# Norm products of the gate and value weights ordered behind attention scores, their squares in four buffers, and w_out's word conversion ordered behind the second token group

## The chip, the core and the metric

The kernel runs on one core of a Trainium2 chip. The metric is the device time of one execution in microseconds. Three runs of the kernel before took 2195.69, 2197.92 and 2199.4 us; their median is 2197.92 us.

## The reference, cut to what matters

Three stages follow one another. The second stage's weights arrive as float64 words in memory (each value is a pair of 32-bit words) and have to be turned into float32 first.

```python
scores = scale * (q @ k.T)                       # 4 batches, 8 heads, 576 x 576, head width 64
scores = where(scores >= max - tau, scores, -1e9)
x = softmax(scores) @ v                          # 2304 tokens x 512

xn = x / rms(x) * rms_g
x = (silu(xn @ w_gate) * (xn @ w_val)) @ w_out   # 512 -> 1536 -> 512

P = sinkhorn(exp(x @ moe2_w_gate), 8 rounds)     # 2304 x 8 experts
out = sum over e of P[:, e] * (relu(x @ w1[e]) @ w2[e])   # 512 -> 1024 -> 512
```

## The kernel before, in words

**Attention.** A batch has 36 tiles: four query groups of 128 rows times 8 heads, and four tiles that hold the 64 remaining rows of two heads each. `att_tile` computes one tile's scores on PE (line 282, four matmuls of 288 columns into one of two PSUM buffers), takes the row maximum on DVE (line 292), the exponential on ACT (line 296), mask and sum on DVE (line 298), splits the result into two 16-bit halves on ACT and POOL (lines 303 to 305), and has SP transpose them by DMA (line 307). Three tiles later `att_values` multiplies the transposed tile with v on PE (line 330); an ordering edge holds these matmuls behind the newest scores. After eight tiles `end_main` divides by the sums (line 376) and `finish_x` normalises the token group, ending with line 353 on DVE; the group, 128 tokens, is then transposed by DMA into `xnT`.

**Preparing the gate and value weights.** When the second token group (number 1) is finished in program order, which is at tile 18, the program emits `prep_group` three times. Each calls `prep_in` for w_gate and for w_val, so there are six calls of four blocks (128x512) each, 24 blocks in all. Per block, `words` loads the 64-bit words by DMA, `to_f32` joins them (ACT line 432, DVE lines 433, 435, 436), ACT squares the result (line 456) and PE multiplies the squares with the squared gains (line 457) to get column norms. The fourth product of a call closes the sum; DVE takes its maximum (line 459), a scale follows, and the four blocks are converted to two 16-bit halves (ACT line 465, DVE line 466). The blocks wait in `stage`, three areas of four blocks that share memory with `wo`, so call number n+3 reuses the area of call n. The squares use tag `u`, two buffers.

**Preparing w_out.** `prep_out` loads 12 blocks of words into the tags `x2` and `x2t`, one buffer each, in turn; `to_f32` joins them (the DVE instructions write the tile `wol`), ACT squares and sums them (line 490). When all 12 are done a common scale is found, and DVE, ACT and POOL write the two halves block by block (lines 507, 508, 509).

**MLP.** A pair of token groups j goes through `mlp_in(j)` (line 530, 288 matmuls for 12 hidden blocks, each followed by ACT line 538, DVE lines 539 and 540, ACT line 544, POOL line 545) and `mlp_out(j)` (line 561, 72 matmuls against `wo`). There are nine pairs. The hidden tiles `tT` have four buffers, of which one pair takes three.

**What sets the order.** Each engine executes its instructions in one fixed order. A scheduler finds the orders ahead of time: it simulates the engines and at each point takes the instruction of the best priority whose inputs are there in its simulation. Priority follows the program's order, except that `attention_order` lifts attention ahead: tiles up to 18 come before the weights' preparation, later tiles come behind `prep_group` but before `mlp_in(0)`, `prep_out` and `mlp_out(0)`. `tc.issue_after(ins)` adds order edges only: each instruction traced in the block that runs on the engine of `ins` has to come behind `ins` in that engine's order. Instructions of other engines in the block are not held.

**After attention** the second expert stage runs (lines 860, 906 and 921), from 679 us to the end.

Of the kernel before, what the change touches and what calls it, by code (L numbers as in the profile page):

```python
# [7 lines left out]
F32 = mybir.dt.float32  # L8
F16 = mybir.dt.float16
BF16 = mybir.dt.bfloat16  # L10
I32 = mybir.dt.int32
AF = mybir.ActivationFunctionType
ALU = mybir.AluOpType
# [6 lines left out]
def kernel(  # L20
# [24 lines left out]
    V, A, G, T = nc.vector, nc.scalar, nc.gpsimd, nc.tensor  # L45
    B, H, S, D = q.shape
    NT, DM = out.shape
    DFF = moe_w_gate.shape[1]
    E, _, FF = moe2_w1.shape
    P = 128  # L50
    KD = DM // P
# [9 lines left out]
    def small(shape, name, dt=F32, bufs=1):  # L61
        return p0.tile(shape, dt, tag=name, name=name, bufs=bufs)
# [43 lines left out]
    gsq = small([P, KD], "gsq", BF16)  # L106
# [16 lines left out]
    HD = DM // 2  # L123
# [17 lines left out]
    pw = pw_cm.__enter__()  # L141
# [124 lines left out]
    HS = S // 2  # L266

    waiting = []
    LAG = 3

    def att_tile(st, c, heads, slot, group):

        kT = st["kT"]
        qT, qX = st["q", c]
        nm = f"{st['b']}_{c}_{heads[0]}"
        sums = group["sums"]
        sp = psa.tile([P, 2, 512], F32, tag="S", name=f"S{nm}", bufs=2)
        rows = P // len(heads)
        for qq, first in ((qT, True), (qX, False)):
            for i, h in enumerate(heads):  # L280
                for j in range(2):
                    last = T.matmul(  # L282
                        sp[i * rows : (i + 1) * rows, j, 0:HS],
                        lhsT=qq[:, h, 0:rows],
                        rhs=kT[h // H2][:, h % H2, j * HS : (j + 1) * HS],
                        start=first,
                        stop=not first,
                    )
        sv = sp[:, :, 0:HS]
        nt = pa.tile([P, 3], F32, tag="nt", name=f"nt{nm}", bufs=4)  # L290
        mx = nt[:, 2:3]
        V.tensor_reduce(mx, sv, AX.XY, ALU.max)
        A.activation(nt[:, 0:1], mx, AF.Copy, scale=st["wt"][:, c : c + 1])
        e = pa.tile([P, S], F32, tag="e", name=f"e{nm}", bufs=3)
        ev = e.rearrange("p (a n) -> p a n", a=2)
        A.activation(ev, sv, AF.Exp, bias=nt[:, 0:1], scale=st["c2"][:, c : c + 1])  # L296
        A.activation(nt[:, 1:2], mx, AF.Identity, bias=st["bt"][:, c : c + 1])
        V.scalar_tensor_tensor(  # L298
            ev, sv, nt[:, 1:2], ev, ALU.is_ge, ALU.mult, accum_out=sums[:, slot : slot + 1]
        )  # L300

        hl = pa.tile([P, 2 * S], F16, tag="hl", name=f"hl{nm}", bufs=3)
        A.activation(hl[:, 0:S], e, AF.Copy)  # L303
        G.tensor_tensor(hl[:, S + REM :], e[:, 0 : NCH * P], hl[:, 0 : NCH * P], ALU.subtract)  # L304
        G.tensor_tensor(hl[:, S : S + REM], e[:, NCH * P :], hl[:, NCH * P : S], ALU.subtract)
        eT = pa.tile([P, 2 * S // P, P], F16, tag="eT", name=f"eT{nm}", bufs=3)
        nc.sync.dma_start_transpose(out=eT, in_=hl)
        waiting.append((st, heads, slot, group, eT))
        if len(waiting) > LAG:

            with tc.issue_after(last.ins):
                att_values(*waiting.pop(0))
# [25 lines left out]
        return rs  # L338

    xnT = {}  # L340

    def finish_x(i, x, ivx):

        ssq = pa.tile([P, 1], F32, tag="ssq", name=f"ssq{i}", bufs=2)
        xn = pa.tile([P, 2, DM], F16, tag="xn", name=f"xn{i}", bufs=1)
        A.activation(xn[:, 0, :].bitcast(BF16), x, AF.Square, scale=ivx, accum_out=ssq)
        ms = pa.tile([P, 1], F32, tag="ms", name=f"ms{i}", bufs=2)
        V.tensor_scalar(ms, ssq, 1.0 / DM, 1e-6, ALU.mult, ALU.add)
        rs = pa.tile([P, 1], F32, tag="rs", name=f"rs{i}", bufs=2)
        G.tensor_tensor(rs, ms, mhalf, ALU.pow)  # L350
        V.tensor_scalar(rs, rs, 16.0, ivx, ALU.mult, ALU.mult)
        A.activation(xn[:, 0, :], x, AF.Copy, scale=rs[:, 0:1])
        V.scalar_tensor_tensor(xn[:, 1, :], x, rs[:, 0:1], xn[:, 0, :], ALU.mult, ALU.subtract)
        j, o = i // 2, (i % 2) * P
        if o == 0:
            xnT[j] = pw.tile([P, 2 * KD, 2 * P], F16, tag="xnT", name=f"xnT{j}", bufs=2)
        nc.sync.dma_start_transpose(
            out=xnT[j][:, :, o : o + P], in_=xn.rearrange("p l d -> p (l d)")
        )
# [49 lines left out]
    wo32 = wo.rearrange("p k l f -> p k (l f)").bitcast(F32)  # L409
# [14 lines left out]
    def to_f32(dst, word, name):  # L424

        lw = pw.tile([P, 2, 2, HD], F16, tag="xs", name=name, bufs=2)  # L430
        lw = lw.rearrange("p o l n -> p (o l n)").bitcast(I32)
        A.activation(dst, word[:, :, 1].bitcast(F32), AF.Copy, scale=2.0**-112)
        V.tensor_scalar(lw, word[:, :, 0], 29, None, ALU.logical_shift_right)
        di = dst.bitcast(I32)
        V.scalar_tensor_tensor(lw, di, 3, lw, ALU.logical_shift_left, ALU.bitwise_or)
        V.scalar_tensor_tensor(
            di, word[:, :, 1], -(2**31), lw, ALU.bitwise_and, ALU.bitwise_or
        )
        return lw

    staged = [0]

    def prep_in(src, w, gi, name):

        bits = src.bitcast(I32)
        raw = stage[:, staged[0] % 3]
        staged[0] += 1
        ps = psm.tile([P, DM], F32, tag="mm", name=f"{name}n{gi}")
        cols = slice(gi * DM, (gi + 1) * DM)
        for kk in range(KD):  # L450
            wd = words(
                bits[kk * P : (kk + 1) * P, 2 * gi * DM : 2 * (gi + 1) * DM], f"{name}w{gi}_{kk}"
            )
            to_f32(raw[:, kk], wd, f"{name}l{gi}_{kk}")
            sq = pw.tile([P, 2 * P], F32, tag="u", name=f"{name}q{gi}_{kk}", bufs=2).bitcast(BF16)
            A.activation(sq, raw[:, kk], AF.Square)
            T.matmul(ps, lhsT=gsq[:, kk : kk + 1].to_broadcast([P, P]), rhs=sq, start=kk == 0, stop=kk == KD - 1)
        n2 = small([P, 1], name + "n2", bufs=2)
        V.tensor_reduce(n2, ps, AX.X, ALU.max)
        s, inv = norm_scale(n2, 1, 9, f"{name}{gi}")  # L460
        gs = small([P, KD], f"{name}gs{gi}")
        V.tensor_scalar(gs, g_sb, s[:, 0:1], None, ALU.mult)
        for kk in range(KD):
            sk, hi = gs[:, kk : kk + 1], w[:, 0, kk, cols]
            A.activation(hi, raw[:, kk], AF.Copy, scale=sk)
            V.scalar_tensor_tensor(w[:, 1, kk, cols], raw[:, kk], sk, hi, ALU.mult, ALU.subtract)
        return inv
# [14 lines left out]
    def prep_out():  # L482

        bits = moe_w_out.bitcast(I32)
        n = KF // NG
        om = small([P, KF], "om")
        for f in range(KF):
            wd = words(bits[f * P : (f + 1) * P, :], f"wo{f}", ("x2", "x2t")[f % 2])
            sq = to_f32(wo32[:, f], wd, f"wol{f}").bitcast(BF16)[:, 0:DM]
            A.activation(sq, wo32[:, f], AF.Square, accum_out=om[:, f : f + 1])  # L490
        for _ in range(2):
            V.tensor_tensor(
                om.rearrange("p (g f) -> p g f", g=NG),
                om.rearrange("p (g f) -> p g f", g=NG),
                igv.to_broadcast([P, NG, n]),
                ALU.mult,
            )
        om1 = small([P, 1], "om1")
        V.tensor_reduce(om1, om, AX.X, ALU.max)
        s, inv = norm_scale(all_max(om1, "womx"), 1, 9, "wout")  # L500
        V.tensor_scalar(ixs, inv, 2.0**10, None, ALU.mult)
        sf = small([P, NG], "wosf")
        V.tensor_scalar(sf, igv, s[:, 0:1], None, ALU.mult)
        rr = pw.tile([P, 4, HD], F32, tag="x2", name="wof")
        for f in range(KF):
            r = rr[:, f % 2 * 2 : f % 2 * 2 + 2].rearrange("p o d -> p (o d)")
            V.tensor_scalar(r, wo32[:, f], sf[:, f // n : f // n + 1], None, ALU.mult)
            A.activation(wo[:, f, 0, :], r, AF.Copy)
            G.tensor_tensor(wo[:, f, 1, :], r, wo[:, f, 0, :], ALU.subtract)
# [108 lines left out]
    for b in range(B):  # L618
        for c in range(NW):
# [4 lines left out]
            i = tiles.index((b, c)) if c < NCH else tiles.index((b, None)) if b % 2 else None  # L624
# [4 lines left out]
    def prepare(b, o):  # L629

        st = states[b]
        if o < NCH * H and o % H == 1:
            prep_q(st, o // H + 1)
        if b > 0 and o in (LAG - 3, LAG - 1):
            prep_v(st, (o - LAG + 3) // 2)
        if b + 1 == B:
# [33 lines left out]

    for t in range(len(row) + LAG):
        before = tc.cur_priority
# [14 lines left out]
        for g in done:  # L687
            i = g["i"]
# [292 lines left out]
```

## Time and profile before

| | us |
|---|---|
| median of three runs | 2197.92 |
| profiled execution, its own time | 2195.02 |
| span of its instructions | 2193.2 |
| PE busy, x13872 matmuls | 2032.0 (93%) |
| DVE busy | 1490.2 (68%) |
| ACT busy | 870.9 (40%) |
| POOL busy | 471.0 (21%) |

The busy times are unions of the instructions' spans on an engine, over the whole span. Shares over the whole span hide that the stages differ, so the prediction reads stretches of the first 600 us. The times of the rows below count from the first instruction of the span.

### The profile page before, as it was taken

How to read it: one execution, taken by the hardware profiler on the slowest of the kernel's cores; microseconds unless marked ns; L12 is line 12 of the kernel's file. 1: busy time of each engine (PE TensorE's matmuls, PEld its weight loads, DVE VectorE, ACT ScalarE, POOL GpSimd, SP SyncE). 2: the span in 40 equal slices, each digit the busy share in tenths (PEclk: the TensorE clock that was granted, in tenths of full speed). 3: DMA queues.
4: the chain of work that ended last, by engine and by line, in shares of the span. 5: the costliest groups of instructions: out<-in, count | busy, mean ns of one | idle time of the engine just before them, and what ended most of it. 6: DMA issues, size and time to landing. Idle time of an engine off the chain costs nothing.

```text
span 2193.2 us, 35334 instructions
## 1 busy us (share of the span) xinstructions
PE 2032.0 (93%) x13872; PEld 1194.7 (54%) x13872; DVE 1490.2 (68%) x3026; ACT 870.9 (40%) x1774; POOL 471.0 (21%) x572
## 2 busy tenths in 40 slices
PE   1358789899999999999999999999999999999999
PEld 0236667666876755545555555555555555555554
DVE  6999677777744287865775765766757757666554
ACT  6878778877843243311221221222212212222111
POOL 1347556665743231000000000000000000000000
PEclk9859999999999999999999999999999999999999
DMA  9895879867826051000100100100001001000001
GB/s 267 207 201 100 169 145 174 159 144 115 147 55 142 18 144 40 29 30 1 39 20 20 39 20 20 39 20 20 20 20 39 20 20 39 20 20 1 1 28 60
DMA packets 321879, 154.10 MB, mean 70 GB/s; under 512 B 278960, under 2 KB 292400, under 8 KB 321712
## 3 DMA queue, kind: packets, MB, share of 16 engines
q1 hardware_dynamic: 321120, 151.82, 30.4%
q8 instruction: 108, 1.77, 0.3%
q14 instruction: 59, 0.48, 0.1%
q0 software_dynamic: 64, 0.00, 0.0%
q10 hardware_dynamic: 528, 0.02, 0.0%
HBM read 68.18 MB, written 12.98 MB: 37 GB/s over the span
## 4 chain that ended last, share of the span: by engine, by line
PE 70%; DVE 2%; DMA 1%; SPq 1%; POOL 0%; issue 0%; ACT 0%; DVEq 0%; ACTq 0%
PE y L906 33%; PE h L860 28%; PE gv L530 5%; PE x L561 2%; PE pv L330 1%; DMA w1r<-in_moe_w_dram 1%; SPq L762 0%; PE S L282 0%; DMA x2T<-x2d 0%; DVE w L714 0%; DMA w2r<-in_moe_w_dram 0%; DMA eT<-hl 0%; PE logits L804 0%; DVE w1m L725 0%; POOL xh L601 0%
## 5 line engine op out<-in xcount | busy, mean ns | idle before, releaser
L860 PE MATMUL h<-x2T,w 128*128 128x384 f16 x4032 | 703.8, 326 | 9.9 <-DMA x2T<-x2d 3.9
L860 PEld LDWEIGHTS <-w 128*128 128x128 f16 x4032 | 394.1, 98 | 300.0 <-issue 14.2
L921 DVE SCALAR_TENSOR_TENSOR acc<-y,coef,acc 128x512 f32<-128x512 f32 x270 | 198.1, 746 | 283.0 <-PE y L906 282.9
L730 POOL TENSOR_TENSOR w1s<-w1r 128x512 f32<-128x512 f32 x16 | 20.3, 1271 | 1060.3 <-DMA w1r<-in_moe_w_dram 1006.3
L304 POOL TENSOR_TENSOR hl<-e,hl 128x512 f16<-128x512 f32 x144 | 172.8, 1200 | 228.2 <-ACT hl L303 146.2
L906 PE MATMUL y<-w,hD 128*128 128x512 f16 x864 | 219.9, 379 | 0.0
L906 PE MATMUL y<-w,hA 128*128 128x512 f16 x864 | 210.6, 379 | 0.9 <-DVE acc L921 0.6
L906 PE MATMUL y<-w,hC 128*128 128x512 f16 x864 | 210.0, 379 | 0.2 <-ACT acc L917 0.2
L906 PE MATMUL y<-w,hB 128*128 128x512 f16 x864 | 210.0, 379 | 0.0
L848 ACT ACTIVATE hA<-u 128x384 f16<-128x384 f32 x96 | 50.2, 522 | 341.1 <-DVE u L876 320.9
L848 ACT ACTIVATE hB<-u 128x384 f16<-128x384 f32 x96 | 50.2, 523 | 312.1 <-DVE u L880 311.2
L530 PE MATMUL gv<-xnT,wg 128*128 128x256 f16 x1296 | 167.8, 278 | 4.5 <-DVE u L540 3.0
L530 PE MATMUL gv<-xnT,wv 128*128 128x256 f16 x1296 | 167.5, 275 | 0.0
L330 PE MATMUL pv<-vs,eT 128*128 128x64 f16 (+1 forms) x2240 | 103.1, 201 | 50.3 <-DMA eT<-hl 47.3
L561 PE MATMUL x<-wo,tT 128*128 128x512 f16 x648 | 144.4, 379 | 1.0 <-DVE u L540 0.9
L906 PEld LDWEIGHTS <-hB 128*128 128x128 f16 x864 | 84.5, 98 | 101.9
L530 PEld LDWEIGHTS <-wg 128*128 128x128 f16 x1296 | 126.5, 100 | 24.0 <-issue 4.1
L298 DVE SCALAR_TENSOR_TENSOR e<-S,nt,e 128x576 f32<-128x576 f32 x144 | 116.3, 809 | 32.0 <-ACT e L296 31.5
L906 PEld LDWEIGHTS <-hD 128*128 128x128 f16 x864 | 84.6, 98 | 95.4
L530 PEld LDWEIGHTS <-wv 128*128 128x128 f16 x1296 | 126.4, 99 | 16.0 <-issue 0.2
L906 PEld LDWEIGHTS <-hC 128*128 128x128 f16 x864 | 84.7, 98 | 91.9 <-issue 0.3
L330 PEld LDWEIGHTS <-eT 128*128 128x128 f16 (+1 forms) x2240 | 91.0, 106 | 79.1 <-DMA eT<-hl 62.1
(244 smaller groups left out, 2852.1 us busy)
## 6 DMA issues: line engine op xcount, KB each, us to landing
w1r<-in_moe_w_dram SPq DMA_DIRECT2D x16, 1024.0 KB, 4.9
w2r<-in_moe_w_dram SPq DMA_DIRECT2D x16, 1024.0 KB, 5.3
wgatew<-in_moe_w_gate_dram SPq DMA_DIRECT2D x12, 512.0 KB, 6.0
wo<-in_moe_w_out_dram SPq DMA_DIRECT2D x12, 512.0 KB, 4.2
wvalw<-in_moe_w_val_dram SPq DMA_DIRECT2D x12, 512.0 KB, 4.5
x2d<-xs SPq DMA_DIRECT2D x24, 256.0 KB, 2.5
qX<-qT SPq DMA_DIRECT2D x40, 128.0 KB, 3.5
raw_k<-in_k_dram SPq DMA_DIRECT2D x4, 1024.0 KB, 6.2
```

The costliest lines, as they stand in the source:

```text
L298: V.scalar_tensor_tensor(ev, sv, nt[:, 1:2], ev, ALU.is_ge, ALU.mult, accum_out=sums[:, slot : slot + 1])
L304: G.tensor_tensor(hl[:, S + REM :], e[:, 0 : NCH * P], hl[:, 0 : NCH * P], ALU.subtract)
L330: T.matmul(o, lhsT=a, rhs=r, start=n == 0, stop=n == len(mm) - 1)
L530: T.matmul(gv[:, a, :], lhsT=w[:, l, kk, f * P : (f + 1) * P], rhs=xt[:, r * KD + kk, :], start=n == 0, stop=n == 3 * KD - 1,)
L561: T.matmul(ps, lhsT=tT[f][:, l, o : o + P], rhs=wo[:, f, r, :], start=n == 0, stop=n == 3 * KF - 1,)
L730: G.tensor_tensor(sm[:, 0], a21, a22, ALU.add)
L848: A.activation(t[:, 0, :], src, AF.Relu)
L860: T.matmul(ps, lhsT=w[:, a, l, kk, f * P : (f + 1) * P], rhs=xb[:, b * 4 + r * 2 + kk, :], start=n == 0, stop=n == 5,)
L906: T.matmul(ps, lhsT=hs[a][f][:, l, jj * P : (jj + 1) * P], rhs=w2[:, r, f, :], start=n == 0, stop=n == 3 * KH - 1,)
L921: V.scalar_tensor_tensor(acc[i], ps, coef[h][:, i : i + 1], acc[i], ALU.mult, ALU.add)
```

## The change

The norm product of block n (n counts 0 to 23 over all six calls) is ordered on PE behind the last score matmul of attention tile 3n//4 + 1: products 0 and 1 behind tile 1, product 3 behind tile 3, product 7 behind tile 6, and so on to product 23 behind tile 18. The squares move from tag `u` to one tile `squares` of four buffers, which takes the tag `x2t`; block kk of each call writes buffer kk. The DVE instructions of w_out's `to_f32` are ordered behind the last DVE instruction of token group 1's `finish_x`.

```diff
+    scored = []
@@ att_tile
         nc.sync.dma_start_transpose(out=eT, in_=hl)
+        scored.append(last.ins)
         waiting.append((st, heads, slot, group, eT))
@@ finish_x
+    normed = {}
-        V.scalar_tensor_tensor(xn[:, 1, :], x, rs[:, 0:1], xn[:, 0, :], ALU.mult, ALU.subtract)
+        normed[i] = V.scalar_tensor_tensor(
+            xn[:, 1, :], x, rs[:, 0:1], xn[:, 0, :], ALU.mult, ALU.subtract
+        ).ins
@@ prep_in
+    squares = pw.tile([P, 4, HD], F32, tag="x2t", name="squares")
+    squared = []
-            sq = pw.tile([P, 2 * P], F32, tag="u", name=f"{name}q{gi}_{kk}", bufs=2).bitcast(BF16)
+            sq = squares[:, kk, :].bitcast(BF16)
             A.activation(sq, raw[:, kk], AF.Square)
-            T.matmul(ps, lhsT=gsq[:, kk : kk + 1].to_broadcast([P, P]), rhs=sq, start=kk == 0, stop=kk == KD - 1)
+            with tc.issue_after(scored[3 * len(squared) // 4 + 1]):
+                T.matmul(ps, lhsT=gsq[:, kk : kk + 1].to_broadcast([P, P]), rhs=sq, start=kk == 0, stop=kk == KD - 1)
+            squared.append(sq)
@@ prep_out
-            sq = to_f32(wo32[:, f], wd, f"wol{f}").bitcast(BF16)[:, 0:DM]
+            with tc.issue_after(normed[1]):
+                sq = to_f32(wo32[:, f], wd, f"wol{f}").bitcast(BF16)[:, 0:DM]
             A.activation(sq, wo32[:, f], AF.Square, accum_out=om[:, f : f + 1])
```

## Rows read from the trace of the kernel before

**Rows 1.** Engines' busy time by stretch; columns as the first line names them.
```profile
core 0: us, PE busy (x) PEld busy (x) DVE busy (x) ACT busy (x) POOL busy (x), PEclk, DMA share, GB/s
...
25.00:152.00 127.00, 51.01 (x372) 27.40 (x372) 121.37 (x261) 105.03 (x213) 40.29 (x42) 0.79 0.87 214
152.00:225.00 73.00, 63.42 (x649) 47.34 (x647) 66.48 (x151) 56.12 (x134) 50.11 (x59) 0.95 0.65 121
225.00:250.00 25.00, 16.32 (x189) 11.74 (x188) 16.72 (x42) 17.36 (x34) 8.01 (x11) 0.86 0.83 194
250.00:600.00 350.00, 324.92 (x3634) 250.10 (x3632) 261.66 (x614) 277.90 (x649) 222.68 (x306) 0.98 0.80 147
```

**Rows 2.** PE's waits, 20 to 152 us: us in total, times, longest.
```profile
PE wgaten L457 <- ACT wgateq L456: 24.5, 10, 9.4
...
PE wvaln L457 <- ACT wvalq L456: 11.9, 7, 4.7
```

**Rows 3.** PE's timeline around two late norm products: start, us, instruction, idle before it.
```profile
108.08 1.11 PE L457 MATMUL wvaln<-wvalq,gsq 128*128 128x512 bf16 x2 [3.01 <-ACT wvalq L456]
110.43 0.64 PE L282 MATMUL S<-kT,qT 128*128 128x288 f16 x2 [1.25 <-DVE e L298]
```

**Rows 4.** DVE's groups by line, 100 to 152 us: busy us, mean ns, idle before.
```profile
L436 DVE SCALAR_TENSOR_TENSOR wo<-wo,wol 128x512 int32<-128x512 int32 x8 | 6.2, 779 | 0.0
...
L435 DVE SCALAR_TENSOR_TENSOR wol<-wo,wol 128x512 int32<-128x512 int32 x8 | 5.4, 678 | 0.0
L433 DVE TENSOR_SCALAR wol<-wo 128x512 int32<-128x512 int32 x9 | 4.7, 524 | 3.1 <-DMA wo<-in_moe_w_out_dram 3.1
```

**Rows 5.** The same groups of DVE, 152 to 225 us.
```profile
L436 DVE SCALAR_TENSOR_TENSOR wo<-wo,wol 128x512 int32<-128x512 int32 x4 | 4.2, 1060 | 0.0
L435 DVE SCALAR_TENSOR_TENSOR wol<-wo,wol 128x512 int32<-128x512 int32 x4 | 3.6, 896 | 0.3 <-ACT wo L432 0.3
...
L433 DVE TENSOR_SCALAR wol<-wo 128x512 int32<-128x512 int32 x3 | 1.3, 422 | 0.8 <-DMA wo<-in_moe_w_out_dram 0.8
```

**Rows 6.** DVE's timeline: the last instruction of token group 1.
```profile
151.92 0.79 DVE L353 SCALAR_TENSOR_TENSOR xn<-x,rs,xn 128x512 f16<-128x512 f32 x1
```

**Rows 7.** Instructions of three lines: ns min/median/max, first and last start.
```profile
L433 DVE TENSOR_SCALAR wol<-wo x12: 390/420/1253, 108.4 to 167.2; 128x512 int32<-128x512 int32 x12
...
L507 DVE TENSOR_SCALAR wof<-wo,wosf x12: 473/532/1365, 186.9 to 221.5; 128x512 f32<-128x512 f32 x12
...
L509 POOL TENSOR_TENSOR wo<-wof,wo x12: 1152/1159/1340, 188.4 to 222.7; 128x512 f16<-128x512 f32 x12
```

**Rows 8.** PE's timeline: starts of mlp_in(0), mlp_out(0) and mlp_in(1).
```profile
156.66 2.74 PE L530 MATMUL gv<-xnT,wg 128*128 128x256 f16 x12 [1.36 <-DMA xnT<-xn]
...
210.38 6.20 PE L561 MATMUL x<-wo,tT 128*128 128x512 f16 x28
...
241.98 0.93 PE L330 MATMUL pv<-vs,eT 128*128 128x64 f16 x14 [3.76 <-DMA eT<-hl]
242.72 2.72 PE L530 MATMUL gv<-xnT,wg 128*128 128x256 f16 x12
```

**Rows 9.** DVE's groups by line, 250 to 600 us.
```profile
L298 DVE SCALAR_TENSOR_TENSOR e<-S,nt,e 128x576 f32<-128x576 f32 x100 | 81.0, 811 | 28.4 <-ACT e L296 28.1
L292 DVE TENSOR_REDUCE nt<-S 128x1 f32<-128x576 f32 x99 | 73.5, 752 | 29.1 <-PE S L282 28.4
```

**Rows 10.** PE's groups by line, 250 to 600 us.
```profile
L530 PE MATMUL gv<-xnT,wg 128*128 128x256 f16 x696 | 91.0, 278 | 2.5 <-DVE u L540 2.5
L561 PE MATMUL x<-wo,tT 128*128 128x512 f16 x301 | 68.1, 379 | 0.0
L330 PE MATMUL pv<-vs,eT 128*128 128x64 f16 (+1 forms) x1498 | 65.9, 195 | 18.6 <-DMA eT<-hl 15.9 <-DVE xrem L395 2.2 <-DVE x L376 0.3
L282 PE MATMUL S<-kT,qT 128*128 128x288 f16 (+1 forms) x216 | 41.1, 290 | 3.4 <-DVE e L298 3.3
L282 PE MATMUL S<-kT,qX 128*128 128x288 f16 (+1 forms) x216 | 40.8, 287 | 0.0
```

**Rows 11.** The DMA queue's own waits on SP, 100 to 230 us.
```profile
SPq L421 <- DVE wo L436: 9.3, 5, 4.6
```

## The prediction, made before the changed kernel ran

> **What bounds the kernel now.** I read the engines' busy time by stretch first [rows 1]. The reader is to see two regimes. From 25 to 152 us DVE is busy 121.4 of 127 us (96%) while PE does 51.0 us of work at a mean granted clock of 0.79: DVE sets the pace. From 250 us on PE is busy 324.9 of 350 us (93%) and DVE 75%: PE sets it. Between lie 152 to 225 us (DVE 66.5 of 73, PE 63.4) and a weak stretch, 225 to 250 us, where neither is full (DVE 16.7, PE 16.3 of 25). PE's work is fixed, so the end moves by as much as PE's finished work is ahead or behind at about 250 us, unless a stall is made or saved later. Next I read the waits of PE and a stretch of its timeline, to see whether the products that are moved hold anything up; then DVE's groups by line before and after token group 1 ends, since that is where the moved conversion stands; then first and last starts, for the pace of w_out's chain.
>
> **The norm products held behind scores.** PE waits 24.5 + 11.9 = 36.4 us in front of products, for squares of ACT [rows 2]. That looks like the gain, but it is mostly no loss. At 108.08 us PE waits 3.01 us for a square; the next scores, at 110.43, then wait another 1.25 us for DVE's line 298, which frees their PSUM buffer [rows 3]. PE stood in front of a product while no score was ready, because DVE was late. I cost the hold at 0. The bounds: at best the 36.4 us were all in attention's way, but DVE has only 127 - 121.4 = 5.6 us free there, so no more than 5.6 us can come of it; at worst it costs the same, by the new waits below.
>
> **What the hold adds.** Order edges on PE add no instruction. With four buffers, the square of block n+4 on ACT must wait for product n, which stands behind the scores of tile 3n//4+1; queued behind that square on ACT are the exponentials of later tiles, and behind those DVE's masks and the next scores. ACT is busy 105.0 of 127 us [rows 1], so it has 22 us of room; I take 0 and keep the 5.6 us above as the cost's end. The conversions of early calls (lines 465, 466) move behind tiles 3, 6, 9 and so on. That is a shift inside the DVE-bound stretch, for all but the last call's are still wanted before tile 18; it costs and gains nothing in sum.
>
> **w_out's conversion behind token group 1.** Between 100 us and the last instruction of token group 1 at 151.92 us [rows 6] DVE runs eight of w_out's twelve blocks: 6.2 + 5.4 + 4.7 = 16.3 us [rows 4]. With DVE full, group 1 ends about 15 us earlier (I leave 1.3 us for DVE's waits for words), and mlp_in(0) starts near 142 instead of 156.66 us [rows 8]. It then lasts as long as before (to 210.38, so 54 us) and ends near 196.
>
> These 16.3 us do not go away; they come behind. All twelve blocks are then converted beside attention and mlp_in(0). In place they cost more: means rise from 678 to 896 ns (line 435) and 779 to 1060 ns (line 436), while line 433 falls from 524 to 422 [rows 4, 5]. That is +0.22 + 0.28 - 0.10 = 0.40 us a block, 3.2 us for eight. Ends: 0 (the slow ones of rows 5 were chance) and 4.0 us (without line 433's fall).
>
> The Trainium skill ("SBUF — State Buffer", section "SBUF: two separate sides") says that a DVE instruction with two SBUF inputs and a GpSimd instruction that reads SBUF exclude each other for the whole of the one that came first. Rows 1 agree in direction: POOL is busy 40.3 of 127 us before 152 us and 50.1 of 73 us behind it. By that rule each of the sixteen moved two-input instructions would meet POOL at work 69% of the time and wait about half of line 509's 1159 ns [rows 7]: 16 x 0.69 x 0.58 = 6.4 us, an estimate by that page, and the gain below would be (10.5 - 6.4) / 1.56 x 1.48 = 3.9 us in place of 6.9. I go by the rows.
>
> **When w_out is ready.** Before, the words' first and last start are 58.8 us apart, the last stands 19.7 us before the first line 507, and mlp_out(0) starts 23.5 us after that; the last block is ready at 222.7 + 1.2 = 223.9 us [rows 7, 8]. Started at 137 us with the same pace: last word 196, first line 507 at 215.5, mlp_out(0) at 239, last block at 252.5. So mlp_out(0) is 29 us later than before although mlp_in(0) is 15 us earlier. The cover of that gap (196 to 239 us) is attention, plus a third of mlp_in(1), for which the fourth `tT` buffer is free. Word loads on SP: twelve as before; behind them in SP's queue stand attention's transposes, and the loads' waits for buffers were 9.3 us in five times [rows 11]. The second buffer comes free only after product 23, since the squares hold it. I count 0, with 9.3 us either way as ends, for the loads move rather than multiply.
>
> **The sum.** DVE decides how much is ready for PE by 250 us. Before, 152 to 250 us holds 66.5 + 16.7 = 83.2 us of DVE work in 98 us. With w_out's blocks always at hand to fill DVE, I let it run at the 96% of the first stretch: 93.7 us, 10.5 more. Less the 3.2 us, 7.3 us are left for attention, which costs DVE 0.811 + 0.752 = 1.56 us a tile [rows 9] (ending a group is left out): 4.7 tiles. A tile is (41.1 + 40.8 + 65.9)/100 = 1.48 us of PE [rows 10], so PE is ahead by 6.9 us. The MLP's part is even: before, by 250 us, all 72 products of mlp_out(0) (72 x 0.226 = 16.3 us) and about 7 us of mlp_in(1) are done [rows 8, 10]; after, 11 us of mlp_out(0) since 239 and a third of mlp_in(1), 96 x 0.131 = 12.6 us, so 23.6 against 23.3. Gain 6.9 us: 2195.02 - 6.9 = 2188.1 on the profiled execution (span 2193.2 and 1.8 around it). That execution was 2.9 us under the median of the runs shown, so I name 2197.92 - 6.9 = 2191 us.
>
> **Rivals.** *The whole lead stays.* mlp_in(0)'s 15 us remain in full and the weak stretch fills as well: its PE idles 25 - 16.3 = 8.7 us [rows 1]. Then 2198 - 24 = 2174. For it: PE work per DVE work is best in mlp_in, and PE is nearly full once it starts. Against it: DVE cannot carry attention and twelve more blocks at once.
>
> *Nothing but an exchange.* What group 1 gains, w_out gives back; the weak stretch only moves, say to 196 to 239 us. 2198. For it: DVE's total is unchanged and it is nearly full. Against it: the 8.3 us that DVE has free from 225 to 250.
>
> *Slower: PE stands for w_out.* PE's order is fixed ahead. If mlp_out(0) comes directly behind mlp_in(0), as at 210.38 before, and scores are queued behind it, PE stands from 196 to 239 us. Attention would stand at about tile 31 at 239 us, four tiles short of where it was when mlp_out(0) started before: 29 + 4 x 1.48 = 35 us behind, less the 8.7 us idle that would not come again, 26 us: 2224. With half the scores ahead of it, 13 us: 2211, which I take. It decides from the point at which PE waits for w_out longer than the 15 us of lead. For it: w_out's slow chain of 12 loads through two buffers. Against it: PE's one long wait near mlp_out(0) now, 3.76 us before 241.98, is for a transpose and not for w_out [rows 8], so the order fits the real pace fairly well.
>
> **How the numbers follow.** A measurement of this kernel can tell about 0.2% (4.4 us) from no change. Forecast 0.43 (2184 to 2198: 0.28 of it faster by over 0.2%, 0.15 within), whole lead 0.22 (faster), exchange 0.12 (within), PE standing for w_out 0.23 (slower). Faster 0.50, within 0.27, slower 0.23. The range, 2170 to 2208, takes in the whole lead with 4 us for the transposes, and above 2198 the ends of the small terms (5.6 + 4.0, or the 9.3 of the word loads); it leaves out most of the slow case. The forecast's own range is 2184 to 2198.
>
> **What would show it.** Group 1's line 353 near 137 us, with no `wol` ahead of it on DVE, and mlp_in(0) near 142. The words' conversion from 137 to about 196, lines 435 and 436 near 0.9 and 1.06 us. mlp_out(0) near 239 and a piece of mlp_in(1) ahead of it. DVE over 93 us busy from 152 to 250, and three to six more tiles done by 250 than before. Wrong if the attention before group 1 is no faster (ACT or transposes set the pace, not DVE), if PE idles over 15 us in front of line 561, or if the time saved by 250 us is lost or multiplied between 250 and 600 us, which I took as unchanged.

## The result: slower by 0.55%, and the profile after

After the change six runs took 2204.9 to 2214.26 us, median 2210.24; six runs of the kernel before had the median 2198.28. The ratio is 1.0055, with a 95% interval of 1.0039 to 1.0071. The profiled execution took 2211.55 us (span 2209.8), 16.5 us more than the one profiled before; the medians are 12.0 apart. The forecast was 2191, in a range of 2170 to 2208. Lines behind line 268 of the code have moved by 1 to 12 numbers: scores are now line 283, their maximum 293, w_out's words 438, 440 and 441, its conversion 519 to 521, `mlp_in` 542, `mlp_out` 573.

The windows of the kernel after, columns as in [rows 1]:

```profile
25.00:152.00 127.00, 54.06 (x421) 32.09 (x423) 116.39 (x257) 102.06 (x208) 42.08 (x46) 0.72 0.85 200
152.00:225.00 73.00, 55.31 (x574) 40.69 (x573) 65.23 (x142) 55.29 (x133) 43.87 (x50) 0.95 0.69 149
225.00:250.00 25.00, 16.80 (x145) 9.41 (x144) 17.45 (x42) 16.08 (x30) 9.11 (x11) 0.80 0.61 138
...
200.00:250.00 50.00, 34.30 (x262) 18.61 (x260) 38.61 (x100) 34.05 (x74) 25.73 (x28) 0.83 0.52 110
...
375.00:640.00 265.00, 240.04 (x2656) 179.25 (x2654) 192.81 (x440) 195.42 (x448) 160.21 (x219) 0.97 0.72 135
```

The same two last windows of the kernel before:

```profile
200.00:250.00 50.00, 40.09 (x376) 26.21 (x375) 38.80 (x86) 36.32 (x81) 28.46 (x34) 0.93 0.67 141
...
375.00:640.00 265.00, 251.82 (x2772) 190.96 (x2770) 188.70 (x448) 199.04 (x459) 165.07 (x225) 0.99 0.73 135
```

Up to 152 us PE now gets more done (421 matmuls against 372) with less of DVE. From 200 to 250 us it gets less done, 262 matmuls against 376, and DVE is no busier than before. To put this in one number I gave each matmul the interval at which those of its line follow one another at full clock (0.109 us in mlp_in, 0.216 in mlp_out) and counted the finished ones: PE is 4.1 us ahead of before at 200 us and 5.3 behind at 250, so 9.4 us go in these 50 us. Of these, 5.8 are more idle time of PE (50 - 34.30 against 50 - 40.09); the other 3.6 fit the lower mean granted clock, 0.83 against 0.93. At 375 us PE is 2.9 ahead again, at 625 it is 13.8 behind, and the spans end 16.6 apart. (In e3, e7, e8 and e12 below, which take as long as before, the count lies within 4 us of before's at these four points.)

The first of the moved words on DVE's timeline, behind token group 1's last instruction (columns as in [rows 6]):

```profile
142.31 0.91 DVE L356 SCALAR_TENSOR_TENSOR xn<-x,rs,xn 128x512 f16<-128x512 f32 x1
...
143.15 1.82 DVE L438 TENSOR_SCALAR wol<-wo 128x512 int32<-128x512 int32 x2
```

Their groups, 142 to 225 us (columns as in [rows 4]):

```profile
L441 DVE SCALAR_TENSOR_TENSOR wo<-wo,wol 128x512 int32<-128x512 int32 x12 | 12.1, 1010 | 0.0
L440 DVE SCALAR_TENSOR_TENSOR wol<-wo,wol 128x512 int32<-128x512 int32 x12 | 10.6, 879 | 0.0
L438 DVE TENSOR_SCALAR wol<-wo 128x512 int32<-128x512 int32 x12 | 6.7, 565 | 2.8 <-DMA wo<-in_moe_w_out_dram 2.8
```

First and last starts, 60 to 250 us, as in [rows 7]; the last line is the maximum from which k's scale for batch 1 is made:

```profile
L438 DVE TENSOR_SCALAR wol<-wo x12: 414/428/1371, 143.2 to 199.8; 128x512 int32<-128x512 int32 x12
...
L519 DVE TENSOR_SCALAR wof<-wo,wosf x12: 448/474/1383, 210.3 to 230.8; 128x512 f32<-128x512 f32 x12
...
L521 POOL TENSOR_TENSOR wo<-wof,wo x12: 1152/1156/1447, 212.6 to 233.1; 128x512 f16<-128x512 f32 x12
...
L180 DVE TENSOR_REDUCE kmm<-km x1: 141/141/141, 104.1 to 104.1; 128x1 f32<-128x3 f32 x1
```

PE's timeline, as in [rows 8]:

```profile
148.16 2.08 PE L542 MATMUL gv<-xnT,wg 128*128 128x256 f16 x9 [0.47 <-DMA xnT<-xn]
...
206.14 0.23 PE L131 MATMUL womxp<-ident,om 128*128 128x128 bf16 x1 [0.34 <-DVE om L511]
207.07 0.22 PE L131 MATMUL kmxp<-ident,kmm 128*128 128x128 bf16 x1 [0.70 <-DVE womx L133]
...
212.54 1.01 PE L573 MATMUL x<-wo,tT 128*128 128x512 f16 x2 [4.48 <-ACT wo L520]
```

The reader is to see that `kmxp`, whose input `kmm` is there at 104.2 us, runs 103 us later, directly behind `womxp`. Both turn a column into a row through one PSUM buffer, tag `mx`, and turns at it go in program order. Before, the two ran at 178.12 and 183.49:

```profile
178.12 0.22 PE L131 MATMUL womxp<-ident,om 128*128 128x128 bf16 x1
...
183.49 0.22 PE L131 MATMUL kmxp<-ident,kmm 128*128 128x128 bf16 x1
```

So in both kernels batch 1's keys cannot be scaled before w_out's words are done. DVE's maxima of scores show what that does. After (the first line is batch 0's last tile, the second batch 1's first two):

```profile
203.59 0.75 DVE L293 TENSOR_REDUCE nt<-S 128x1 f32<-128x576 f32 x1
236.18 1.42 DVE L293 TENSOR_REDUCE nt<-S 128x1 f32<-128x576 f32 x2
```

And before:

```profile
206.52 0.76 DVE L292 TENSOR_REDUCE nt<-S 128x1 f32<-128x576 f32 x1 [0.24 <-PE S L282]
227.79 1.41 DVE L292 TENSOR_REDUCE nt<-S 128x1 f32<-128x576 f32 x2
```

Batch 0's attention ends 2.9 us earlier and batch 1's starts 8.4 us later: 32.6 us without a tile in place of 21.3. In that hole PE has little but mlp_out(0), and that waits for w_out, as its waits from 150 to 250 us show (before has no wait on `wo` there):

```profile
PE pv L332 <- DMA eT<-hl: 6.9, 5, 1.8
PE x L573 <- ACT wo L520: 5.2, 2, 4.5
PE S L283 <- DVE xm L582: 4.1, 1, 4.1
...
PE x L573 <- POOL wo L521: 2.5, 5, 0.9
```

### The profile page after: what moved, and what is told of

Its sections match the earlier page's. It is cut to its first block, busy times and chain, and to the rows that moved or that the text cites. A ratio compares the mean times of both kernels' runs of the same rounds, so it can differ in the third digit from the quotient of the medians.

```text
span 2209.8 us, 35299 instructions
## 1 busy us (share of the span) xinstructions
PE 2035.2 (92%) x13871; PEld 1196.0 (54%) x13872; DVE 1495.7 (68%) x3026; ACT 871.8 (39%) x1774; POOL 472.1 (21%) x572
## 4 chain that ended last, share of the span: by engine, by line
PE 69%; DVE 2%; DMA 1%; POOL 1%; issue 0%; ACT 0%; SPq 0%; ACTq 0%; DVEq 0%
PE y L918 33%; PE h L872 28%; PE gv L542 5%; PE x L573 2%; DMA w2r<-in_moe_w_dram 1%; DMA x2T<-x2d 0%; PE pv L332 0%; DVE w L726 0%; DMA w1r<-in_moe_w_dram 0%; DMA eT<-hl 0%; DVE xn L356 0%; SPq L774 0%; PE logits L816 0%; PE S L283 0%; POOL xh L613 0%
## 5 line engine op out<-in xcount | busy, mean ns | idle before, releaser
L542 PEld LDWEIGHTS <-wv 128*128 128x128 f16 x1296 | 127.1, 99 | 16.7 <-issue 0.5
L918 PEld LDWEIGHTS <-hA 128*128 128x128 f16 x864 | 84.4, 98 | 90.3 <-issue 2.3
```

The lines of the kernel that those rows point to most:

```text
L542: T.matmul(gv[:, a, :], lhsT=w[:, l, kk, f * P : (f + 1) * P], rhs=xt[:, r * KD + kk, :], start=n == 0, stop=n == 3 * KD - 1,)
L918: T.matmul(ps, lhsT=hs[a][f][:, l, jj * P : (jj + 1) * P], rhs=w2[:, r, f, :], start=n == 0, stop=n == 3 * KH - 1,)
```

## The experiments

The table gives for each run the ratio to the kernel before with its 95% interval and, from its trace, when `womxp` ran, when mlp_out(0) began and ended, and when the first maximum of batch 1 was taken (us).

| | ratio | womxp | mlp_out(0) | batch 1 |
|---|---|---|---|---|
| before | 1 | 178 | 210 to 230 | 228 |
| after | 1.0055 [1.0039, 1.0071] | 206 | 213 to 238 | 236 |
| e1_products | 1.0052 [1.0040, 1.0064] | 204 | 211 to 233 | 237 |
| e2_wout | 1.0067 [1.0054, 1.0081] | 211 | 216 to 241 | 239 |
| e3_buffers | 0.9996 [0.9986, 1.0005] | 184 | 216 to 235 | 237 |
| e4_wout_behind0 | 1.0034 [1.0022, 1.0046] | 183 | 220 to 240 | 234 |
| e5_after_own_bank | 1.0114 [1.0096, 1.0132] | 234 | 244 to 278 | 211 |
| e6_before_own_bank | 1.0089 [1.0074, 1.0105] | 217 | 229 to 263 | 215 |
| e7_products_two | 0.9985 [0.9971, 0.9999] | 184 | 210 to 226 | 229 |
| e8_late_placebo | 0.9999 [0.9988, 1.0010] | 182 | 214 to 234 | 232 |
| e9_hold_half | 1.0034 [1.0021, 1.0047] | 198 | 210 to 234 | 235 |
| e10_after_keys | 1.0041 [1.0026, 1.0056] | 205 | 211 to 237 | 235 |
| e11_after_loadq | 1.0025 [1.0014, 1.0036] | 208 | 214 to 240 | 238 |
| e12_before_keys | 0.9997 [0.9987, 1.0007] | 181 | 213 to 232 | 230 |
| e13_before_light | 0.9977 [0.9966, 0.9989] | 182 | 209 to 228 | 228 |
| e14_after_light | 0.9951 [0.9936, 0.9966] | 177 | 200 to 221 | 219 |
| e15_wout_later | 1.0090 [1.0068, 1.0112] | 222 | 225 to 248 | 249 |
| e16_two_half | 1.0046 [1.0028, 1.0064] | 179 | 219 to 240 | 227 |
| e17_before_short | 0.9959 [0.9944, 0.9974] | 170 | 205 to 225 | 221 |
| e18_after_short | 1.0016 [1.0006, 1.0026] | 197 | 203 to 228 | 225 |

**The parts one by one.** e1_products is before with the held products and the four squares in `x2t`, but w_out not held:

```diff
+    squares = pw.tile([P, 4, HD], F32, tag="x2t", name="squares")
-            sq = pw.tile([P, 2 * P], F32, tag="u", name=f"{name}q{gi}_{kk}", bufs=2).bitcast(BF16)
+            sq = squares[:, kk, :].bitcast(BF16)
+            with tc.issue_after(scored[3 * len(squared) // 4 + 1]):
                 T.matmul(ps, lhsT=gsq[:, kk : kk + 1].to_broadcast([P, P]), rhs=sq, ...
```

> Norm products held behind scores with the squares in four buffers; w_out's conversion as before. Theory W (w_out's late conversion makes PE wait at mlp_out(0) and sets batch 1's k preparation back, and that costs the 12 us): 2193 to 2200, no wait of PE on w_out's blocks. Theory P (the held products set attention back): 2206 to 2214. Theory R (the loss arises from 375 to 625 us, where nothing was changed, because the orders there were planned anew): any time from 2190 to 2215, and the lag against the kernel before grows behind 375 us, not ahead of it.

e2_wout is before with w_out's words alone held; e4_wout_behind0 holds them behind group 0 (`normed[0]`) instead:

```diff
+            with tc.issue_after(normed[1]):
                 sq = to_f32(wo32[:, f], wd, f"wol{f}").bitcast(BF16)[:, 0:DM]
```

> Only w_out's DVE conversion held behind token group 1; products and squares as before. Theory W: 2206 to 2214, PE waits 5 to 10 us on w_out's blocks between 200 and 240 us. Theory P: 2193 to 2200. Theory R: any time from 2190 to 2215; the wait on w_out's blocks is there but is made good by 375 us as in the changed kernel.

> w_out's DVE conversion held behind token group 0 (ends at 116 us; unheld it starts at 108 us), so only one or two of its blocks are moved. Theory W: within 4 us of the kernel before. Theory P: the same. Theory R: the small edge is enough to plan later orders anew, and it may move by 5 to 15 us either way.

e3_buffers is e1 without the `issue_after` line.

> Only the squares in four buffers in tag x2t, no order edge. Theories W and P: within 4 us of the kernel before (2194 to 2202), as nothing is held. Theory R: the orders are planned anew here too, so it may move by 5 to 15 us either way.

Each hold costs alone about what both cost together (by the ratios 11 and 15 us, against 12), and buffers alone cost nothing. In e3 batch 1 starts as late as in after (237 us) and nothing is lost: that date by itself is not the price. In e1 nothing holds w_out by an edge, yet `womxp` is at 204: the word blocks that go through `x2t` wait until the squares leave it, behind product 23: that product runs at 129.8 us, and the second block's load is issued at 130.4 (in before at 16.6). (So e1 cannot tell theory W from theory P; its time lies in P's range.) mlp_out(0) waits there too:

```profile
203.64 0.22 PE L131 MATMUL womxp<-ident,om 128*128 128x128 bf16 x1
...
210.56 1.01 PE L567 MATMUL x<-wo,tT 128*128 128x512 f16 x2 [3.44 <-ACT wo L514]
```

Two edits with one effect do not add, so what they share is the suspect: w_out's lateness. e4 does not fit; its `womxp` was on time, and it is told of below.

**Is it the queue for the buffer `mx`?** e5_after_own_bank and e6_before_own_bank give `womxp` a buffer in the tag `mm`, in the kernels after and before:

```diff
-        ps = psm.tile([P, P], F32, tag="mx", name=name + "p", bufs=1)
+        if name == "womx":
+            ps = psm.tile([P, DM], F32, tag="mm", name=name + "p")[:, 0:P]
+        else:
+            ps = psm.tile([P, P], F32, tag="mx", name=name + "p", bufs=1)
```

> The changed kernel, but the product that spreads w_out's maximum over the partitions (womxp) takes a buffer of tag mm instead of the single buffer mx, which the maxima of batch 1's k and v need too. Theory M (w_out's late scale holds that buffer's turn, so batch 1's key maximum, ready near 105 us, is multiplied only at 207 us, its keys are converted from 210 and tile 36 starts at 236): kmxp far ahead of womxp, batch 1's keys converted before 180 us, tile 36 under 220 us, no lag of PE work against the kernel before at 225 to 275 us, 2190 to 2204. Theory W (PE's wait for w_out's blocks at mlp_out(0) is the loss): tile 36 and the lag stay, 2206 to 2214. Theory R (orders behind 375 us planned anew): the lag at 275 us may go, but 5 to 10 us are lost behind 375 us, 2200 to 2212.

> The kernel before with the same edit to womxp. Theory M: kmxp far ahead of 183 us, tile 36 under 222 us instead of 228, and the time 2185 to 2196. Theory W: no change beyond 4 us. Theory R: 2188 to 2212.

PE's timeline of e5:

```profile
104.22 0.29 PE L134 MATMUL kmxp<-ident,kmm 128*128 128x128 bf16 x1 [7.33 <-DVE kmm L183]
...
234.19 0.31 PE L134 MATMUL womxp<-ident,om 128*128 128x128 bf16 x1
...
244.25 2.34 PE L576 MATMUL x<-wo,tT 128*128 128x512 f16 x5
```

And of e6, whose mlp_in(0) ends at 216.8 us:

```profile
216.39 0.39 PE L533 MATMUL gv<-xnT,wv 128*128 128x256 f16 x2
216.62 0.22 PE L134 MATMUL womxp<-ident,om 128*128 128x128 bf16 x1
```

The dependency is real: with its own buffer k's row comes at 104 us and batch 1's tiles at 211. But both kernels became slower than any theory said (0.6% over after, 0.9% over before), since the edit made w_out later still. In e5 the last load of words is issued at 221.9 us on SP, behind batch 1's loads and transposes (the eleventh at 194.9). In e6 the words end as before and their maximum is there at 180.9 us, but `womxp` now takes its turn in tag `mm` among the hidden blocks of mlp_in(0), and runs at that stage's end. So the two do not say what batch 1's late start costs while w_out is on time. They show that a late w_out costs even when batch 1 is early, which turns the suspicion on w_out and mlp_out(0) themselves.

**The hold without the late words.** e7_products_two is e1 with the squares left in the two buffers of `u`.

> Products held behind scores, but the squares stay in tag u with two buffers, so x2t is free for w_out's words from the start; w_out's conversion not held. Theory M (in the run with held products alone, w_out came late because the squares sat in x2t until the last product): womxp near 180 us instead of 204, tile 36 near 228 instead of 237, no lag at 275 us, 2192 to 2203. Theory P (the hold itself delays attention): lag of 5 us at 275 us as with four buffers, 2206 to 2214. Theory R: as M until 375 us, then 5 to 10 us lost.

```profile
183.66 0.22 PE L131 MATMUL womxp<-ident,om 128*128 128x128 bf16 x1
...
209.88 2.32 PE L566 MATMUL x<-wo,tT 128*128 128x512 f16 x10 [0.69 <-ACT wo L513]
```

These rows of e7 answer to e1's above: the same hold, w_out on time, and 0.9985 in place of 1.0052. Holding the products costs nothing by itself; e1 lost by the squares' place, in which the hold keeps them (without the hold, in e3, the same place cost nothing).

**Chance of the orders.** Any edit makes the scheduler plan anew. e8_late_placebo moves q's scale by one tile from batch 1 on; the orders came out as before's, so it is a repeat. e10_after_keys and e12_before_keys move the second half of the keys, from batch 1 on, in after and before; e11_after_loadq moves q's load in after (the labels behind # are added here):

```diff
-        if o == 28:   # e8
+        if o == (28 if b == 0 else 29):
-        if o == 34:   # e10, e12
+        if o == (30 if early else 34):
-        if o == 25:   # e11
+        if o == (23 if early else 25):
```

> The kernel before; only from batch 1 on, the next batch's q scales are prepared one tile later (after tile 29 instead of 28), which is some 270 us at the earliest, and is work of 5 squares on ACT. Theories M, W and P: within 4 us of the kernel before. Theory R (an order planned anew costs 5 to 10 us by itself): 2202 to 2210, the lag growing behind 375 us.

> The changed kernel; only, from batch 1 on, the second half of the next batch's keys is prepared four tiles earlier, so all orders are the same up to about 290 us and planned anew behind it. Theory W (the loss is owed to what is late by 250 us): 2206 to 2215 again. Theory R (what is lost behind 375 us, 17 us in the one trace, hangs on the order planned there and not on what was changed): 2194 to 2204, or anywhere else, with the lag at 250 us as before.

> The kernel before with the keys' second half four tiles earlier from batch 1 on, orders the same up to about 300 us and planned anew behind it. Theory W: within 4 us of the kernel before, 2194 to 2203, since w_out is as early as before. Theory R: 5 to 15 us away from it, because the order behind 300 us decides.

> The changed kernel; only, from batch 1 on, the next batch's q is loaded two tiles earlier, so PE's order is the same up to about 430 us and planned anew behind it. Theory W: 2206 to 2215 again. Theory R: what is lost behind 430 us (14 us in the one trace) comes out differently, 2196 to 2206 or over 2216.

e9_hold_half is e1 with two products to a tile in place of one and a third (`len(squared) // 2 + 1`), so the last stands behind tile 12.

> Products held behind scores with four buffers in x2t as in the run of held products alone (2209.5), but the last product behind tile 12 instead of 18, so x2t comes free some 25 us earlier; w_out's conversion not held. Theory W (how late w_out's scale is decides: womxp at 178 to 184 us in the kernels of 2196 to 2205 us, at 204 to 211 in those of 2209 to 2211, at 217 to 234 in those of 2219 to 2224): womxp near 185 to 192 us and 2194 to 2204 us. Theory P (the hold with four buffers costs by itself): 2206 to 2213. Theory R: no relation to womxp, 2194 to 2214.

Orders that are the same up to some 290 us (e10) or 430 us (e11, on PE) and differ behind give back 3 and 7 us of the 12, but both stay slower than before with intervals clear of 1. e11's interval lies clear of after's, e10's does not. So part of the loss hangs on the later orders; 0.25 to 0.41% stays with these two. Their traces repeat the early loss: 11.1 and 9.2 us by the count from 200 to 250 us, where after lost 9.4 and e8 and e12 lost 1.8 and 0.5. e9 frees `x2t` earlier, `womxp` comes at 198 and the loss is 0.34% in place of 0.52; its 2205.06 us lies between the ranges of W and P. Its words end at 175 us and their maximum is there at 180, but PE's order has `womxp` 18 us behind that.

**Is w_out's lateness the cause?** e13_before_light and e14_after_light leave lines 433, 435 and 436 out for w_out in before and after (its values are then ACT's copy of the high words, and the squares use tag `xs`); e15_wout_later puts the words of before later than the change does, behind hidden block 5 of mlp_in(0); e16_two_half is e7 with e9's index.

```diff
-                sq = to_f32(wo32[:, f], wd, f"wol{f}").bitcast(BF16)[:, 0:DM]   # e13, e14
+            sq = pw.tile([P, 2, 2, HD], F16, tag="xs", name=f"wol{f}", bufs=2)
+            ...
+            A.activation(wo32[:, f], wd[:, :, 1].bitcast(F32), AF.Copy)
+            with tc.issue_after(hidden_ins[0, 5]):   # e15
+                sq = to_f32(wo32[:, f], wd, f"wol{f}").bitcast(BF16)[:, 0:DM]
```

> The kernel before without the three DVE instructions per block that join w_out's words (lines 433, 435, 436; w_out's values are then not the reference's), 25 us of DVE less, so w_out is ready earlier. Base of the pair with the next run. Theory W: womxp near 150 to 165 us, 2185 to 2196 us. Theory R: 2185 to 2210.

> The changed kernel without the same three instructions: products held, four buffers in x2t, but nothing of w_out on DVE that an edge could hold. Theory W (w_out's lateness is the cause): womxp by 185 us, and no slower than the run before it by more than 4 us, rather faster by the lead of 4 to 6 us at 175 us. Theory P (the holds themselves cost): 8 to 14 us slower than it. Theory R: no telling, but a lag that arises behind 375 us.

> The kernel before with w_out's DVE conversion ordered behind the sixth hidden block of mlp_in(0), near 180 us, so w_out is about 30 us later than in the changed kernel; products and squares as before. Theory W: mlp_out(0) ends at 260 to 275 us and the time is 2216 to 2226. Theory R: no more than the 2202 to 2212 of the other held kernels.

> Held products with the squares in u (two buffers), the last product behind tile 12 instead of 18; w_out not held. Theory W: w_out on time (womxp by 186 us), so 2193 to 2200. Theory R: 2193 to 2212 without relation to womxp.

e14 keeps the products' hold and the squares in `x2t`, but the hold of the words has nothing left to act on. It is 5 us faster than e13 (2188.33 and 2193.47); PE's timeline has `womxp` and mlp_out(0) earlier than before:

```profile
176.98 0.22 PE L131 MATMUL womxp<-ident,om 128*128 128x128 bf16 x1
...
199.83 3.62 PE L574 MATMUL x<-wo,tT 128*128 128x512 f16 x16
```

e15 goes the other way; PE stands 18.4 us for the words, and 20 us are lost:

```profile
221.52 0.29 PE L131 MATMUL womxp<-ident,om 128*128 128x128 bf16 x1 [18.36 <-DVE om L500]
```

By the count e14 is 3.0 us ahead of e13 at 225 us, where after was 4.8 behind before. At 250 it is 1.5 behind (PE stands 7.05 us for one transpose), so the 5 us by which it wins arise later. In e13 `womxp` came at 182 us, not at 150 to 165, and in e15 mlp_out(0) ended at 248, not at 260 to 275. Taking the lateness away takes most of the early loss away, more of it raises the price. The count says so for all kernels: from 200 to 250 us the nine others with `womxp` by 184 us end between 2.7 us behind and 3.4 ahead of before, and of the ten with `womxp` at 197 us or later eight lose 7.7 to 17.9 us. The other two are e9 (2.9) and e6 (2.4, and 9.4 more by 275; its mlp_out(0) ends at 263). So w_out's lateness is the cause that the runs show for the loss from 200 to 250 us. How that loss divides between PE's waits at mlp_out(0) and the missing tiles of batch 1 they do not show. e16 is a miss. Its words are on time and it is 0.46% slower all the same. In it and in e4 mlp_in(0) ended late (218 and 216 us, 206 in after), so mlp_out(0) ended at 240; but by the count of finished work they are only 0.9 and 2.7 us behind before at 250 us, and 9.5 and 7.3 at 625. Their loss arises later, and whether more than the chance of later orders is in it is not settled.

**A version that beats both.** e17_before_short and e18_after_short make every float32 word with two DVE instructions in place of three, for all 36 blocks, in before and after. The three lowest of the 23 mantissa bits are then zero, which leaves 20.

```diff
-        V.tensor_scalar(lw, word[:, :, 0], 29, None, ALU.logical_shift_right)
-        V.scalar_tensor_tensor(lw, di, 3, lw, ALU.logical_shift_left, ALU.bitwise_or)
+        V.tensor_scalar(lw, di, 3, None, ALU.logical_shift_left)
```

> The kernel before, with the low word of each weight left out (lines 433 and 435 become one shift, so the three lowest of 23 mantissa bits are zero): two DVE instructions per block in place of three, some 0.7 us less in each of 36 blocks, 24 us in all, most of it in the stretch where DVE is full. Theory W: mlp_in(0) near 140 us, mlp_out(0) ends by 215 us, 2178 to 2190. Theory R: 2178 to 2205.

> The changed kernel with the same edit. Theory W (the holds cost only through w_out's lateness, which is now 8 us less late of the 12 blocks' own work): mlp_out(0) ends 5 to 8 us later than in the run before it, and the time is 4 to 10 us over it, 2184 to 2198. Theory R: no telling within 2180 to 2205.

e17 is 9 us faster than before (its mlp_out(0) ended at 225 us, not by 215). Under it the change costs 13 us (2188.95 to 2201.85), as much as without it; theory W had said 4 to 10, and 2201.85 is over its range. Windows of e17, then of e18:

```profile
152.00:200.00 48.00, 42.96 (x542) 36.45 (x540) 43.71 (x113) 41.28 (x102) 34.70 (x43) 1.00 0.61 125
200.00:250.00 50.00, 43.15 (x396) 29.04 (x394) 36.51 (x87) 36.79 (x80) 28.95 (x36) 0.93 0.70 156
```

```profile
152.00:200.00 48.00, 41.91 (x474) 34.46 (x471) 40.75 (x104) 41.06 (x103) 27.86 (x35) 0.96 0.90 184
200.00:250.00 50.00, 35.93 (x271) 20.05 (x271) 36.03 (x81) 34.29 (x73) 25.96 (x29) 0.80 0.61 138
```

The whole difference of this pair arises from 200 to 250 us, 396 against 271 matmuls, and stays: by the count of finished work e18 is level with e17 at 200 us, 10.5 us behind at 250 and 11.8 at the end.

## Why the prediction was wrong

**Group 1 earlier: right, smaller.** It ended at 142.3 us and mlp_in(0) started at 148.2 (forecast 137 and 142). The lead of mlp_in(0) was 8.5 us and not 15; DVE's busy time up to 152 us fell from 121.4 to 116.4, and I had it full.

**The words' price and pace: right.** A block cost 0.565 + 0.879 + 1.010 = 2.45 us against 2.38 forecast; they ran from 143 to 200 (137 to 196). Eight moved blocks so cost 8 x (2.45 - 1.98) = 3.8 us more, with 1.98 from [rows 4]; the forecast was 3.2. The estimate by the Trainium skill ("SBUF — State Buffer", section "SBUF: two separate sides") was 6.4.

**The hold at 0: right for the edges (e7), wrong for the tag.** The prediction saw that the squares keep `x2t` until product 23, and counted 0 with 9.3 us as the end. It makes the difference of 0.67% between e7 and e1: the load that waits for it makes w_out late.

**DVE at 96% through 250 us: the step that failed.** I took 93.7 us of DVE work from 152 to 250; it was 65.23 + 17.45 = 82.7, hardly other than before's 83.2; from 200 to 250 us DVE was busy 38.61 of 50 (77%). The reason given was that w_out's blocks are always at hand and attention takes what is left. But between 200 and 250 us neither is at hand: the last of the words' conversions begins at 199.8, then the chain of om, `womxp` and the scale has to pass before a block can be converted, and behind `womxp`, through the one buffer `mx`, stand k's scale, the keys, and batch 1's first tile at 236. By 250 us four tiles of batch 1 had their maximum, before six; three to six more were forecast. I had weighed the words as load on DVE and not as the head of two chains. With what was measured, my sum gives (82.7 - 83.2 - 3.8) / 1.56 x 1.48 = -4.1 us, near the 5.3 that PE is behind at 250.

**mlp_out(0) at 239: wrong.** It began at 212.5, 2.2 us behind the first line 519, since the 19.7 and 23.5 us between the words' end and mlp_out(0) in [rows 7, 8] were no fixed distance: PE had been in mlp_in(0) until 209.4. After, it ran on the heels of the conversion and stood 5.2 + 2.5 = 7.7 us for blocks.

**The slower rival** gave 2211 and the right place, but not the right way: PE was to stand over 15 us in front of line 561, with scores queued behind. It stood 7.7, there were no scores to hold up, and by 250 us only 5.3 us were lost. That its time came so near is luck.

**Nothing lost behind 250 us: wrong.** In after's profile the 5.3 us are made good by 375 and then 16.7 are lost to 625, a term that the prediction put at nothing without a reason. Part of that is in waits of PE (375 to 640 us): for transposes 13.4 us against 7.9, for DVE's `u` 9.6 against 2.5. e11 shows that part of it hangs on later orders. That the early loss is gone for a while and another comes stays open: in e18 the same early loss simply stayed, and one profile of each is not enough to part the two.

## What to carry to other kernels

A conversion moved behind other work frees its place only if nothing waits for its end: before moving it, follow from its last instruction every buffer that has one place and is handed out in program order, for an unrelated chain (here the next batch's keys) may stand in that queue. Putting scratch into a tag that a later stage loads through is such a hold too, with no edge in the code to show it. A change to an order planned ahead needs controls: here an edit whose orders differ only from 430 us on (e11) moved the time by 7 us of 2200, and two kernels with w_out on time (e4, e16) were 0.34 and 0.46% slower.

## What the hardware showed unexpectedly

In after's trace one DVE instruction, whose median in the same trace is 0.93 us, lasted 4.56 us:

```profile
571.08 4.56 DVE L356 SCALAR_TENSOR_TENSOR xn<-x,rs,xn 128x512 f16<-128x512 f32 x1 [0.36 <-ACT xn L355]
```

Through nearly all of it POOL ran six instructions with no gap between them, the last ending 0.6 us before it:

```profile
571.04 0.68 POOL L557 TENSOR_TENSOR tT<-u,tT 128x256 f16<-128x256 f32 x1
571.67 0.68 POOL L613 TENSOR_TENSOR xs<-x2t,xs 128x256 f16<-128x256 f32 x1
572.30 1.16 POOL L305 TENSOR_TENSOR hl<-e,hl 128x512 f16<-128x512 f32 x1
...
574.78 0.31 POOL L306 TENSOR_TENSOR hl<-e,hl 128x64 f16<-128x64 f32 x1
```

PE waited for what stood behind it on DVE, which is half of its 9.6 us of waits for `u` above:

```profile
577.02 2.72 PE L542 MATMUL gv<-xnT,wg 128*128 128x256 f16 x12 [4.75 <-DVE u L552]
```

By the Trainium skill ("SBUF — State Buffer", section "SBUF: two separate sides"), a DVE instruction with two inputs in SBUF and a POOL instruction that reads SBUF exclude each other. The trace agrees in kind: both inputs of line 356 are in SBUF. If that is what held it, DVE stood here not for one POOL instruction but for a whole run of them; no run takes POOL's work away to test it. The same instruction lasted 3.57 us once in e10 and 2.31 once in e18; in e11, 7 us faster than after, it never lasted over 1.29.
